# Four rooms for a result tile, a wider step between weight units, and a last sweep in two passes, in a single-core attention and two-layer kernel

## The chip, the cores and the metric

The kernel runs on one core of a Trainium2 chip. The metric is the device time of one execution in microseconds (us), and the number to predict is the median over a few runs. The core has a matrix engine (TensorE, PE in the rows, with its weight loads listed apart as PEld), a vector engine (VectorE, DVE), a scalar engine (ScalarE, ACT), GpSimd (POOL) and SyncE (SP). SyncE computes nothing here; nearly all DMA transfers are issued from its queue (SPq), in the order in which the program writes them, and an issue that has to wait holds back all issues behind it.

## The reference

Attention over 4 batches of 576 tokens and 8 heads of 64 (the first four heads see a band of 32 tokens, the others every 32nd token), and then two small networks on the 2304 tokens:

```python
x = attention(q, k, v)                      # 2304 x 512
h = ((x @ w1) * (x @ w2)) @ w3              # d_ff 1024
y = h @ w_out                               # 2304 x 512
h2 = y @ w_in                               # 2304 x 2048
g = h2 * (1.0 / (1.0 + np.exp(-1.702 * h2)))
out = (g @ w_out2).astype(np.float32)       # 2304 x 512
```

All weights arrive as 8-byte floats.

## The kernel before

**Arithmetic.** Every product of fp32 matrices is made of three matrix multiplications: each factor is split into a rounded part ("hi", written by ScalarE in `split_hi`, L246) and the rest ("lo", written by VectorE in `split_lo`, L252), and `ORDER` lists the three pairs that are multiplied. The product w3 @ w_out is formed once, so y is (a*b) times one matrix. The second network is computed by a scheme with seven block products in place of eight: `win` and `wout` are cut into eight units, the sums of their blocks are formed on the chip and stored in DRAM (`widram` and `tdram`).

**Order.** Four long lists of steps are written by hand. Each step has a number, `written()` sorts a list by these numbers, and what results is the program order of TensorE, VectorE, ScalarE and SyncE. The numbers are places, not times: the engines run as far ahead as their waits for each other allow, each strictly in its own order.

**The third list** (`steps3`, roughly 335 to 437 us) is where most of the change lies. One unit of its numbers is one half piece on TensorE: `one(0)` or `one(1)` in `pieces()`, 12 multiplications (L716) for a 128-column block m of x @ w1 or x @ w2. After `one(0)`, ScalarE copies the result (L1234, `abf<-ps`); after `one(1)`, VectorE multiplies it in (L1237); then ScalarE and VectorE split the product into hi and lo (`ab`). The results of `one` live in the pool `mm`, which has four buffers, so that the half piece four places on needs the copy or the multiplication to be done. For the last of the four batches 16 half pieces (half batch 0), the products for y (`fourth()`, L1354), 16 half pieces (half batch 1) and again `fourth()` follow each other.

Ahead of these stand the last y products of batch 2 (`y_products`, L1173, four tiles n = 0 to 3). `y_out` copies each of the four results to a tile `ysb` (ScalarE, L1181) and stores it (SyncE, L1182). `y_out` takes a tuple of pools, and each pool has two rooms for `ysb`:

```python
ysb = where[n % len(where)].tile([P, HB], F32, tag="ysb", name="ysb", bufs=2)
nc.scalar.activation(ysb, yacc[n], AF.Copy)
nc.sync.dma_start(ydram[n, :, s * HB:(s + 1) * HB], ysb)
```

Between the pieces ScalarE and VectorE do two other jobs. `y_steps` (L1324, L1329 and splits into `yq`) forms the seven block sums of y for the first third of the tokens. `wo_steps` converts one unit of `wout`: two ScalarE steps (L1144, L1145), three VectorE steps (L1146 to L1148), three sums (L1133, L1093, L1133), two ScalarE and two VectorE splits, and two stores of 896 KB each to `tdram` (L1128). Unit 0 goes through `early_room` (tile `x`) with `late` = 1.6, at the end of the second list; units 1 to 6 follow in the third list and use the two halves of `sums` by turns, so a unit waits for the stores of the unit two before it; unit 7 is done in the fourth list. `wo_load` (L1389) loads a unit, 1 MB, into one of three rooms.

**The fourth list** (`steps4`, from 437 us to the end) works on three blocks of 768 tokens. Each has eight `Quad`s, in which the products y @ w_in are made, and then, in `after()`, five sweeps over eight chunks (`piece`, L1508: per chunk three token tiles of 128, three multiplications each). Each sweep takes 8 x 9 multiplications; the split parts come from `Split`, a ring of seven buffers `sp`. The sum of a sweep lies in two PSUM tiles: the first holds token tiles 0 and 1 (512 columns), the second token tile 2 (256 columns). `Out` copies the two or adds them to a room `ob` (L1524, L1529), and `put` stores 384 KB (L1533).

Of the kernel before, what the change touches and what calls it, by code (L numbers as in the profile page):

```python
# [212 lines left out]
def body(ctx: ExitStack, tc, qk, vv, mask, ql, vl, qs, vs, qmask, w1, w2, w3t, wo, win, wout, out):  # L213
# [906 lines left out]
    def wo_steps(u, raw, room, high_room=None, late=0):  # L1120
# [18 lines left out]
        def high(n):  # L1139
# [9 lines left out]
            (2.65, lambda: sum_(S1, B12, B22, ALU.add)),  # L1149
            (2.75, lambda: both_minus(room()[:, 5 * 256:7 * 256], part(B11), room())),  # L1150
            (3.1, lambda: sum_(B12, B21, S2, ALU.add)),
# [101 lines left out]
    for hb in range(2):  # L1253
        for m in range(MC):
            steps2 += pieces(2, hb, m, hold)
        for n in range(KC):
            at_ = 24 * hb + 2 * MC + 2 * n
            todo_ = steps2 if hb == 0 else over
            for half in range(2):
                ks = list(range(4 * half, 4 * half + 4))  # L1260
                todo_.append((at_ + half, lambda hb=hb, n=n, ks=ks: y_products(hb, n, ks)))
            todo_.append((at_ + 1.99, lambda hb=hb, n=n: y_out(4 + hb, n, (p1,))))
# [6 lines left out]
    cv_a = None  # L1269
# [121 lines left out]
    UNIT = 7.2  # L1391
    for u in range(1, NU):
        at = -5.8 if u == 1 else 6 + UNIT * (u - 2)
        if 1 < u < NU - 1:
            steps3.append((((2.6, 5.5, 5.7)[u - 2] if u < 5 else at - 10), lambda u=u: wo_load(u)))
        if u < NU - 1:
            steps3 += [(at + g, f) for g, f in wo_steps(u, lambda u=u: todo3[u], lambda u=u: sums[:, u % 2])]
# [60 lines left out]
    class Split:  # L1458

        def __init__(self, src):  # L1460
            self.src = src

        def hi(self):
            self.t = p2.tile([P, 2, HT], F32R, tag="sp", name="sp", bufs=7)
# [37 lines left out]
    def piece(acc, b, j, i, g, opens=False):  # L1502

        t3 = factor[b, j, i // 2]
        for t in range(HT // P):
# [9 lines left out]
    class Out:  # L1515
# [15 lines left out]
        def put(self, b, right, d):  # L1531
            c0 = b * BT + right * HT
            nc.sync.dma_start(out[c0:c0 + HT, d * 256:d * 256 + 256].rearrange("(t p) n -> p t n", p=P), self.t)  # L1533
# [90 lines left out]
    def after(b, q, X, Y):  # L1624
# [4 lines left out]
        sp = [Split(lambda n=n, i=i: parts[i][:, SWEEP[n][1]]) for n, i in order]  # L1629
        D(PC * 2, piece, Y, b, B21, NU - 1, q.a12, True)  # L1630
        for s, (n, i) in enumerate(order):
            D(PC * pos[s] + 0.01, piece, (X, Y)[n % 2], b, SWEEP[n][0], i, sp[s], n == 1)
# [5 lines left out]
            else:  # L1638
                D(PC * (pos[s] - 3) + 0.1, sp[s].hi)
                D(PC * (pos[s] - 3) + 0.65, sp[s].lo)  # L1640
        D(PC * 3 + 0.02, t_more, 2)
        c11, u1, z1, c22, c21, c12 = (Out() for _ in range(6))
        for n in range(2):
# [6 lines left out]
            D(PC * 41 + 0.02 + 0.01 * n, c12.copy, X, n)  # L1650
# [3 lines left out]
        D(PC * 41 + 0.1, c12.put, b, 0, 1)  # L1654
# [101 lines left out]
```

## Time and profile before

| | |
|---|---|
| median of three runs | 799.18 us (797.74 to 799.43) |
| the profiled execution | 799.78 us |
| span of the profiled execution, first to last instruction | 798.0 us |
| TensorE busy | 771.7 us of the span (97%) |
| VectorE busy | 580.8 us (73%) |
| ScalarE busy | 480.2 us (60%) |
| mean granted TensorE clock, share of full | 0.998 |
| DMA traffic | 168.14 MB, mean 211 GB/s |

The span leaves out 1.78 us of the profiled execution that lie around the first and the last instruction. All times within the execution are counted from the start of the span. TensorE is busy nearly all the time, so what counts is where it is not, and at which clock it runs.

### The profile page before, as it was taken

To read this page: it belongs to the slowest core of one execution; us is meant where nothing else is said; L and a number is where in the kernel's file an instruction comes from. 1 tells how busy PE (TensorE), PEld (TensorE's weight loads), DVE (VectorE), ACT (ScalarE), POOL (GpSimd) and SP (SyncE) were. 2 spreads that over 40 slices of the span, in tenths; PEclk is the share of its full clock that TensorE was granted. 3 is DMA by queue.
4 is the path that set the end of the run, shared out by engine and by line. 5 is a ranking of instruction groups with operands and counts; after the bars stand their busy time and mean duration, and the time that the engine had idled before them with its cause. 6 is when DMAs were issued, how large, how long until landed. Compare 5 with 4: busy or idle time off the path is not lost.

```text
span 798.0 us, 16759 instructions
## 1 busy us (share of the span) xinstructions
PE 771.7 (97%) x6545; PEld 746.6 (94%) x6545; DVE 580.8 (73%) x1248; ACT 480.2 (60%) x1041; POOL 5.8 (1%) x14
## 2 busy tenths in 40 slices
PE   5899999999999999997999999999999999999997
PEld 4889999987999999997989999999999999999997
DVE  4989678788688687967766787795567795577643
ACT  6867646577665545444464667673666673665552
POOL 2000000000000000000000000000000000000000
PEclk9999999999999999999999999999999999999999
DMA  8987455632787545386699936789354489343382
GB/s 261 311 295 240 164 173 185 198 114 82 265 268 278 164 164 217 111 228 212 168 275 261 365 132 204 303 280 361 133 189 166 152 278 364 123 161 108 120 275 82
DMA packets 72062, 168.14 MB, mean 211 GB/s; under 512 B 6320, under 2 KB 45232, under 8 KB 69424
## 3 DMA queue, kind: packets, MB, share of 16 engines
q1 hardware_dynamic: 71840, 167.04, 62.8%
q8 instruction: 51, 0.84, 0.4%
q14 instruction: 27, 0.22, 0.1%
q10 hardware_dynamic: 144, 0.04, 0.0%
HBM read 130.88 MB, written 36.18 MB: 209 GB/s over the span
## 4 chain that ended last, share of the span: by engine, by line
PE 75%; DMA 12%; DVE 6%; ACT 4%; issue 2%; SPq 0%; ACTq 0%; DVEq 0%
PE acc L1508 23%; PE ps L1497 22%; PE ps L716 12%; PE ps L1173 8%; PE acc L1019 5%; DMA raw<-in_w 3%; DMA raw<-in_wout 2%; DMA tdram<-sums 2%; PE acc L1354 2%; DMA ydram<-ysb 1%; DMA vl<-in_vl 1%; PE sc L533 1%; PE pv L602 1%; ACT sm L556 1%; DMA tdram<-raw 1%
## 5 line engine op out<-in xcount | busy, mean ns | idle before, releaser
L1508 PE MATMUL acc<-w,sp 128*128 128x256 f32 x1512 | 188.3, 283 | 0.0
L1508 PEld LDWEIGHTS acc<-w,sp 128*128 128x128 f32 x1512 | 186.5, 191 | 0.1
L1497 PE MATMUL ps<-yq,hl 128*128 128x384 f32 x924 | 168.1, 335 | 0.0
L1497 PEld LDWEIGHTS ps<-yq,hl 128*128 128x128 f32 x924 | 158.7, 188 | 0.9 <-DVE part L1453 0.6
L252 DVE TENSOR_TENSOR sp<-part,sp 128x384 fp32r<-128x384 f32 x144 | 75.3, 552 | 59.9 <-ACT sp L246 59.9
L716 PE MATMUL ps<-xbh,w 128*128 128x288 f32 x512 | 102.6, 295 | 0.8 <-DVE w L252 0.7
L716 PE MATMUL ps<-xah,w 128*128 128x288 f32 x512 | 102.4, 295 | 0.0
L716 PE MATMUL ps<-xal,w 128*128 128x288 f32 x256 | 77.2, 302 | 6.1 <-DVE abf L1237 4.4
L716 PEld LDWEIGHTS ps<-xbh,w 128*128 128x128 f32 x512 | 81.9, 188 | 1.3 <-DVE w L252 1.2
L1173 PE MATMUL ps<-ab,w 128*128 128x288 f32 x576 | 81.0, 300 | 1.8 <-DVE ab L252 1.8
L716 PEld LDWEIGHTS ps<-xah,w 128*128 128x128 f32 x512 | 82.0, 188 | 0.0
L1173 PEld LDWEIGHTS ps<-ab,w 128*128 128x128 f32 x576 | 78.2, 191 | 3.2 <-DVE ab L252 2.2
L716 PE MATMUL ps<-xbl,w 128*128 128x288 f32 x256 | 77.2, 301 | 1.2 <-ACT abf L918 0.8
L246 ACT ACTIVATE sp<-part 128x384 fp32r<-128x384 f32 x144 | 68.2, 518 | 16.4 <-PE acc L1508 15.7
L1450 ACT ACTIVATE part<-part 128x384 f32<-128x384 f32 x72 | 37.9, 526 | 62.2 <-DVE part L1453 62.2
L716 PEld LDWEIGHTS ps<-xal,w 128*128 128x128 f32 x256 | 48.0, 187 | 8.9 <-DVE abf L1237 5.8
L246 ACT ACTIVATE ab<-abf 128x288 fp32r<-128x288 f32 x64 | 27.2, 438 | 44.4 <-DVE abf L1237 40.4
L716 PEld LDWEIGHTS ps<-xbl,w 128*128 128x128 f32 x256 | 48.0, 188 | 2.7 <-ACT abf L918 1.0
L1019 PE MATMUL acc<-w,w 128*128 128x512 f32 x192 | 45.6, 396 | 0.1
L1019 PEld LDWEIGHTS acc<-w,w 128*128 128x128 f32 x192 | 35.8, 188 | 9.2 <-ACT raw L1025 1.0
L252 DVE TENSOR_TENSOR hl<-fetched,hl 128x1024 fp32r<-128x1024 f32 (+1 forms) x40 | 43.2, 1081 | 0.0
L246 ACT ACTIVATE w<-xw 128x512 fp32r<-128x512 f32 (+1 forms) x30 | 23.2, 775 | 29.1 <-DVE xw L809 28.3
(189 smaller groups left out, 1089.1 us busy)
## 6 DMA issues: line engine op xcount, KB each, us to landing
w<-tdram SPq DMA_DIRECT2D x84, 512.0 KB, 4.3
fetched<-widram SPq DMA_DIRECT2D x20, 896.0 KB, 7.4
raw<-in_win SPq DMA_DIRECT2D x8, 1024.0 KB, 5.9
widram<-x SPq DMA_DIRECT2D x8, 896.0 KB, 5.4
raw<-in_wout SPq DMA_DIRECT2D x7, 1024.0 KB, 5.1
tdram<-raw SPq DMA_DIRECT2D x6, 896.0 KB, 6.3
tdram<-sums SPq DMA_DIRECT2D x6, 896.0 KB
raw<-in_w3t SPq DMA_DIRECT2D x10, 512.0 KB, 4.6
```

The source lines that it names most:

```text
L246: nc.scalar.activation(hi, src, AF.Copy)
L252: e.tensor_tensor(lo, src, r(hi), op=ALU.subtract)
L533: nc.tensor.matmul(sc[:nq, g, i * P:i * P + nk], qs[rows, i], ks[rows, i], start=True, stop=True,)
L556: nc.scalar.activation(sm[:nq, h, :nk], sm[:nq, h, :nk], AF.Exp, bias=st[:nq, 0, h:h + 1], scale=-1.0, accum_out=st[:nq, 1, h:h + 1],)
L602: nc.tensor.matmul(pv[rows, h // 2, :nq], L["v"][:nk, h * D:(h + 1) * D], ps[:nk, h * nq:(h + 1) * nq], start=True, stop=True,)
L716: nc.tensor.matmul(ps, ws[a][m // 2][:, at:at + P], xh[c][:, k, cols], start=(k == 0 and (a, c) == ORDER[0]), stop=(k == KC - 1 and (a, c) ...
L1019: nc.tensor.matmul(acc[f], hl[:, a, f * P:(f + 1) * P], wor[c][g], start=(g == 0 and (a, c) == ORDER[0]), stop=(g == MC - 1 and (a, c) == ...
L1173: nc.tensor.matmul(yacc[n], wfs[a][k][:, n * P:(n + 1) * P], hold[s % 2, k][:, c], start=(k == 0 and (a, c) == ORDER[0]), stop=(k == MC - ...
L1354: nc.tensor.matmul(st[0], wfs[a][k][:, n * P:(n + 1) * P], hold[hb, k][:, c], start=(k == 0 and (a, c) == ORDER[0]), stop=(k == MC - 1 and ...
L1450: nc.scalar.activation(out(), src(), func)
L1497: nc.tensor.matmul(ps, w[a][:, f * 256 + kk * P:f * 256 + (kk + 1) * P], yq[:, b, kk, c], start=(first and kk == 0 and (a, c) == ORDER[0]) ...
L1508: nc.tensor.matmul(to, g.t[:, a, t * P:(t + 1) * P], t3[:, i % 2, c], start=(opens and i == 0 and n == 0 and t % 2 == 0), stop=(i == NU - ...
```

## The change

Four edits:

1. The four `y_out` of batch 2's second half batch get the pools `p1` and `cv_b` by turns, so four rooms for `ysb` in place of two.
2. In `wo_steps` the three sums of a unit with `late` (only unit 0, 1.6) get places 0.8 further back.
3. `UNIT`, the distance between two units of `wout` in the third list, is 8.0 in place of 7.2, and the loads of units 5 and 6 stand 14 places ahead of their unit in place of 10.
4. In the last block's last sweep TensorE goes through all eight chunks for token tiles 0 and 1 first, and then through all eight for token tile 2. The eight split parts, which all have to be kept until the end, are written to `yq`, whose contents are no longer needed then, and six chunks ahead in place of three. The first PSUM tile is copied and stored (256 KB) ahead of the end, the second one (128 KB) at the end.

```diff
-            (2.65, lambda: sum_(S1, B12, B22, ALU.add)),
-            (2.75, lambda: both_minus(room()[:, 5 * 256:7 * 256], part(B11), room())),
-            (3.1, lambda: sum_(B12, B21, S2, ALU.add)),
+            (2.65 + late / 2, lambda: sum_(S1, B12, B22, ALU.add)),
+            (2.75 + late / 2, lambda: both_minus(room()[:, 5 * 256:7 * 256], part(B11), room())),
+            (3.1 + late / 2, lambda: sum_(B12, B21, S2, ALU.add)),
...
-            todo_.append((at_ + 1.99, lambda hb=hb, n=n: y_out(4 + hb, n, (p1,))))
+            todo_.append((at_ + 1.99, lambda hb=hb, n=n: y_out(4 + hb, n, (p1, cv_b) if hb else (p1,))))
...
-    UNIT = 7.2
+    UNIT = 8.0
...
-            steps3.append((((2.6, 5.5, 5.7)[u - 2] if u < 5 else at - 10), lambda u=u: wo_load(u)))
+            steps3.append((((2.6, 5.5, 5.7)[u - 2] if u < 5 else at - 14), lambda u=u: wo_load(u)))
...
-            self.t = p2.tile([P, 2, HT], F32R, tag="sp", name="sp", bufs=7)
+            self.t = self.room or p2.tile([P, 2, HT], F32R, tag="sp", name="sp", bufs=7)
...
+        final = b + 1 == NB
+        sp = [
+            Split(lambda n=n, i=i: parts[i][:, SWEEP[n][1]], yq[:, i // 2, i % 2] if final and n == 4 else None) for n, i in order
+        ]
...
+            if final and n == 4:
+                for m, ts in enumerate(((0, 1), (2,))):
+                    D(PC * (33 + (0, 8 * 2 / 3)[m] + i * (2 - m) / 3) + 0.01, piece, X, b, SWEEP[n][0], i, sp[s], False, ts)
...
-                D(PC * (pos[s] - 3) + 0.1, sp[s].hi)
-                D(PC * (pos[s] - 3) + 0.65, sp[s].lo)
+                ahead = 6 if final and n == 4 else 3
+                D(PC * (pos[s] - ahead) + 0.1 + 0.01 * (ahead > 3), sp[s].hi)
+                D(PC * (pos[s] - ahead) + 0.65 + 0.01 * (ahead > 3), sp[s].lo)
...
-            D(PC * 41 + 0.02 + 0.01 * n, c12.copy, X, n)
+            D(PC * (41 - (8 / 3 if final and n == 0 else 0)) + 0.02 + 0.01 * n, c12.copy, X, n)
...
+        if final:
+            D(PC * 41 - 2.5, c12.put, b, 0, 1, 0, 2)
+            D(PC * 41 + 0.1, c12.put, b, 0, 1, 2, 3)
+        else:
+            D(PC * 41 + 0.1, c12.put, b, 0, 1)
```

How edit 2 moves VectorE at the end of the second list (`x` is unit 0; `ab_2714` is the split of the last two blocks, m = 6 and m = 7, of batch 2's second half batch, and each L1237 is the multiplication of one block):

```order
 L1237 TENSOR_TENSOR abf<-ps,abf 128x288
 L252 TENSOR_TENSOR xal<-pv,xah 128x2x96 x2
+L252 TENSOR_TENSOR ab_2714<-abf,ab_2714 128x288
 L1133 TENSOR_TENSOR x<-x 128x256
 L1093 TENSOR_TENSOR x<-x 128x512
 L1133 TENSOR_TENSOR x<-x 128x256
-L252 TENSOR_TENSOR ab_2714<-abf,ab_2714 128x288
 L1237 TENSOR_TENSOR abf<-ps,abf 128x288
 L252 TENSOR_TENSOR ab_2714<-abf,ab_2714 128x288
```

The lo split of block m = 6 moves ahead of the three sums; the multiplication and the split of block m = 7 stay behind them.

How edit 3 moves SyncE's issues, in the third list from the stores of unit 3 on (`raw<-in_wout` are the loads of units 5 and 6; `tdram<-raw` and `tdram<-sums` are the hi and lo stores of units 3 and 5, `tdram<-x` is unit 4's hi store; `w_73` is a block of `w_in`):

```order
-L1128 DMA tdram<-raw 128x7x256
 L1389 DMA raw<-in_wout 128x1024
+L1128 DMA tdram<-raw 128x7x256
 L1128 DMA tdram<-sums 128x7x256
 L1363 DMA ydram<-ysb 128x288 x4
+L1389 DMA raw<-in_wout 128x1024
 L1128 DMA tdram<-x 128x7x256
-L1389 DMA raw<-in_wout 128x1024
-L1128 DMA tdram<-sums 128x7x256
-L1128 DMA tdram<-raw 128x7x256
+L1128 DMA tdram<-sums 128x7x256
```

The load of unit 5 moves ahead of unit 3's hi store, and the load of unit 6 ahead of unit 4's hi store.

How edit 4 moves TensorE at the very end (`w_1624` and `w_1625` are ring buffers with the last factors):

```order
 L1508 MATMUL acc<-w_1627,sp 128x256 x36
-L1508 MATMUL acc<-w_1624,sp 128x256 x36
-L1508 MATMUL acc<-w_1625,sp 128x256 x36
-L1752 UNCONDITIONAL_BRANCH
+L1508 MATMUL acc<-w_1624,yq 128x256 x24
+L1508 MATMUL acc<-w_1625,yq 128x256 x24
+L1508 MATMUL acc<-w_1624,yq 128x256 x12
+L1508 MATMUL acc<-w_1625,yq 128x256 x12
+L1766 UNCONDITIONAL_BRANCH
```

The number of multiplications is the same; a third of them now stands in a second pass. Nowhere else does TensorE's order change.

## Rows read from the trace of the kernel before

**Rows 1.** TensorE in order of time: start, us, instruction, idle time before it

```profile
338.64 0.66 PE L1173 MATMUL ps<-ab,w 128*128 128x288 f32 x3 [1.10 <-DVE ab L252]
339.98 11.71 PE L1173 MATMUL ps<-ab,w 128*128 128x288 f32 x75 [0.67 <-DVE ab L252]
351.53 0.29 PE L716 MATMUL ps<-xal,w 128*128 128x288 f32 x1
...
362.16 0.40 PE L716 MATMUL ps<-xal,w 128*128 128x288 f32 x1 [2.33 <-DVE abf L1237]
...
372.12 0.40 PE L716 MATMUL ps<-xal,w 128*128 128x288 f32 x1 [0.97 <-ACT abf L1234]
...
374.55 0.40 PE L716 MATMUL ps<-xal,w 128*128 128x288 f32 x1 [0.59 <-DVE abf L1237]
...
380.09 0.40 PE L716 MATMUL ps<-xal,w 128*128 128x288 f32 x1 [0.30 <-ACT abf L1234]
```

**Rows 2.** Stretches: length, busy PE, PEld, DVE, ACT, POOL, clock, DMA, GB/s

```profile
341.00:344.00 3.00, 3.00 (x14) 3.00 (x14) 1.88 (x3) 2.49 (x4) 0.00 (x0) 0.50 0.69 196
...
351.50:383.40 31.90, 27.34 (x195) 25.64 (x194) 22.26 (x33) 16.18 (x28) 0.00 (x0) 1.00 0.69 203
...
396.00:424.20 28.20, 26.66 (x196) 25.96 (x195) 20.19 (x32) 14.09 (x24) 0.00 (x0) 1.00 1.01 280
...
436.70:793.80 357.10, 357.10 (x2521) 355.57 (x2519) 247.26 (x407) 217.52 (x400) 0.00 (x0) 1.00 0.61 212
```

**Rows 3.** ScalarE in order of time, 353 to 372 us

```profile
353.65 0.41 ACT L1181 ACTIVATE ysb<-ps 128x288 f32<-128x288 f32 x1 [4.22 <-DMA ydram<-ysb]
...
369.30 1.14 ACT L1144 ACTIVATE raw<-raw 128x1024 int32<-128x1024 uint32 x1 [2.28 <-DMA raw<-in_wout]
...
371.69 0.38 ACT L1234 ACTIVATE abf<-ps 128x288 f32<-128x288 f32 x1
```

**Rows 4.** VectorE in order of time, 338 to 374 us

```profile
338.14 0.45 DVE L252 TENSOR_TENSOR ab<-abf,ab 128x288 fp32r<-128x288 f32 x1
338.51 0.45 DVE L1237 TENSOR_TENSOR abf<-ps,abf 128x288 f32<-128x288 f32 x1
339.47 0.46 DVE L252 TENSOR_TENSOR ab<-abf,ab 128x288 fp32r<-128x288 f32 x1 [0.51 <-ACT ab L246]
...
354.94 1.09 DVE L252 TENSOR_TENSOR sums<-sums,raw 128x896 fp32r<-128x896 f32 x1 [4.38 <-ACT raw L246]
...
361.66 0.45 DVE L1237 TENSOR_TENSOR abf<-ps,abf 128x288 f32<-128x288 f32 x1
...
374.05 0.45 DVE L1237 TENSOR_TENSOR abf<-ps,abf 128x288 f32<-128x288 f32 x1
```

**Rows 5.** The chain of work that ended last: start, us, what

```profile
344.31 9.26 DMA ydram<-ysb
353.96 0.95 ACT raw L246
354.93 5.48 DMA tdram<-raw
360.43 8.77 DMA raw<-in_wout
...
393.01 13.19 DMA tdram<-sums
...
424.16 12.58 PE acc L1354 x96
```

**Rows 6.** Two stretches with little DMA: length, clock, DMA share, GB/s

```profile
376.00:380.00 4.00, 1.00 0.00 0
...
388.00:392.00 4.00, 1.00 0.01 3
```

**Rows 7.** ScalarE's last two copies, in order of time

```profile
793.50 0.87 ACT L1524 ACTIVATE ob<-acc 128x512 f32<-128x512 f32 x2 [6.67 <-PE acc L1508]
```

**Rows 8.** The last stretches, columns as in the second group

```profile
795.00:796.00 1.00, 0.00 (x0) 0.00 (x0) 0.00 (x0) 0.00 (x0) 0.00 (x0) 1.00 0.69 236
796.00:797.00 1.00, 0.00 (x0) 0.00 (x0) 0.00 (x0) 0.00 (x0) 0.00 (x0) 1.00 0.47 158
```

More of the change, by code (lines that the diff above doesn't have):

```diff
@@ L1268, in body @@
     right2 = ExitStack()
-    cv_a = None
+    cv_a = cv_b = None
     early = {}
@@ L1458, in body, with __init__ @@
     class Split:
-        def __init__(self, src):
-            self.src = src
+        def __init__(self, src, room=None):
+            self.src, self.room = src, room
         def hi(self):
-            self.t = p2.tile([P, 2, HT], F32R, tag="sp", name="sp", bufs=7)
+            self.t = self.room or p2.tile([P, 2, HT], F32R, tag="sp", name="sp", bufs=7)
             split_hi(self.t[:, 0], self.src())
@@ L1500, in product, with piece @@
                 )
-    def piece(acc, b, j, i, g, opens=False):
+    def piece(acc, b, j, i, g, opens=False, ts=range(HT // P)):
         t3 = factor[b, j, i // 2]
-        for t in range(HT // P):
+        for t in ts:
             to = acc[t // 2][:, t % 2 * 256:t % 2 * 256 + 256]
@@ L1529, in add, with put @@
             nc.vector.tensor_tensor(self.o[:, WIDE[n]], acc[n][:, :768 - 512 if n else 512], other.o[:, WIDE[n]], op=ALU.add)
-        def put(self, b, right, d):
+        def put(self, b, right, d, lo=0, hi=HT // P):
             c0 = b * BT + right * HT
-            nc.sync.dma_start(out[c0:c0 + HT, d * 256:d * 256 + 256].rearrange("(t p) n -> p t n", p=P), self.t)
+            nc.sync.dma_start(
+                out[c0 + lo * P:c0 + hi * P, d * 256:d * 256 + 256].rearrange("(t p) n -> p t n", p=P), self.t[:, lo:hi]
+            )
     MM, PC = 1.05, 1.07
@@ L1628, in after @@
         pos = [s if s < 2 else s + 1 for s in range(len(order))]
-        sp = [Split(lambda n=n, i=i: parts[i][:, SWEEP[n][1]]) for n, i in order]
+        final = b + 1 == NB
+        sp = [
+            Split(lambda n=n, i=i: parts[i][:, SWEEP[n][1]], yq[:, i // 2, i % 2] if final and n == 4 else None) for n, i in order
+        ]
         D(PC * 2, piece, Y, b, B21, NU - 1, q.a12, True)
         for s, (n, i) in enumerate(order):
-            D(PC * pos[s] + 0.01, piece, (X, Y)[n % 2], b, SWEEP[n][0], i, sp[s], n == 1)
+            if final and n == 4:
+                for m, ts in enumerate(((0, 1), (2,))):
+                    D(PC * (33 + (0, 8 * 2 / 3)[m] + i * (2 - m) / 3) + 0.01, piece, X, b, SWEEP[n][0], i, sp[s], False, ts)
+            else:
+                D(PC * pos[s] + 0.01, piece, (X, Y)[n % 2], b, SWEEP[n][0], i, sp[s], n == 1)
             if i % 2:
@@ L1653, in after @@
         D(PC * 33 + 2.4, c21.put, b, 1, 0)
-        D(PC * 41 + 0.1, c12.put, b, 0, 1)
+        if final:
+            D(PC * 41 - 2.5, c12.put, b, 0, 1, 0, 2)
+            D(PC * 41 + 0.1, c12.put, b, 0, 1, 2, 3)
+        else:
+            D(PC * 41 + 0.1, c12.put, b, 0, 1)
         if b + 1 < NB:
```

## Prediction

> **What bounds the kernel now.** I first read the stretches. From 436.7 us on TensorE is busy for all of 357.1 us at full clock [rows 2], so the fourth list is bound by TensorE, and what starts it earlier ends it earlier by the same amount. The third list is different. Twelve multiplications, a half piece, take 12.58 / 96 x 12 = 1.57 us where nothing waits [rows 5], so 16 of them take 25.2 us. Half batch 0 takes 31.9 us and half batch 1 takes 28.2 us [rows 2]: 6.7 and 3.0 us are waits and restarts. Then I read who ends them. TensorE's own order shows it idle for 2.33, 0.97, 0.59 and 0.30 us ahead of half pieces that need a PSUM buffer back, from a copy (ACT L1234) or a multiplication (DVE L1237) [rows 1]. VectorE and ScalarE lead further back: the multiplication that ended the 2.33 us stood at 361.66 behind work that began after an idle 4.38 us at 354.94 [rows 4], and that waited for ScalarE, which had stood 4.22 us for the store of a `ysb` tile [rows 3]. The chain of waits puts these in one line: store of `ysb` 9.26 us, split, `tdram` store 5.48, load of unit 2 8.77, and later a `sums` store of 13.19 us [rows 5]. So there it is a chain of transfers, not TensorE, that sets the time.
>
> A smaller loss comes earlier: TensorE waits 1.10 and 0.67 us for the lo splits of blocks m = 6 and 7 [rows 1], and from 341 to 344 us the granted clock is 0.50, the level of 1.2 GHz, which costs half of 3.0 us, 1.5 us [rows 2].
>
> **Edit 1, the rooms.** It removes the 4.22 us. The third copy can begin at 353.65 - 4.22 = 349.4; its result is there by then, since the fourth tile's 24 multiplications (3.1 us) end at 351.5 [rows 1], so the third's ended at 348.4. In the built order the second and fourth copies wait for TensorE alone and the third for a store of the half batch before: the new rooms are free. Queued behind the third copy are the split at 353.96, the splits of y, the fourth copy and the first copies of half batch 0; all move 4.2 us. On VectorE the multiplication at 361.66 comes at 357.4 and ends at 357.9. TensorE wants its buffer at 362.16 - 2.33 = 359.8: the 2.33 us are gone.
>
> What is late next is unit 2. Its load waits for unit 1's hi store (same room). That store goes out at 350.7 instead of 354.93; with the same 5.48 and 8.77 us [rows 5] the unit is there at 365.0, where ScalarE took it up at 369.30 after idling 2.28 us [rows 3]. ScalarE's copy of block 3 stands behind the unit's two conversions: 371.69 becomes 367.4, done at 367.8; TensorE, running from 351.53 without waits, wants it after ten half pieces at 367.2, and waits 0.6. The multiplication of block 3, 374.05 [rows 4], becomes 369.8 and ends at 370.2; wanted at 369.4, a wait of 0.8. The copy that released TensorE at 380.09 [rows 1] does so at 375.8; wanted at 370.2 + 3 x 1.57 = 374.9, 0.9. So 2.3 us of the 6.7 remain, and half batch 0 ends about 4.3 us earlier, as much as the transfers move. Bounds: were the store to take the longest landing seen, 13.19 us, the load would come after 369.3 and nothing is won; were both transfers shorter, all 6.7 us. I take the same transfers' own times, 4.3 us, as sizes and neighbours are the same.
>
> **Edit 3, the distance of the units.** In half batch 1 the waits came from unit 5, whose second conversion could not write `sums` until unit 3's store had landed, 393.01 + 13.19 = 406.2 us [rows 5]. That store shared the DMA engines with the load of unit 5, issued just before. Now that load stands ahead of unit 3's stores; it waits only for unit 2's hi store to land, at about 375.1 + 5.5 = 380.6, and the engines are nearly idle then (shares of 0.00 and 0.01 in two stretches [rows 6]). Unit 3's lo store goes out near 393.0 - 4.3 = 388.7 and lands at 394.2 (5.48 us) or 401.9 (13.19 us). Unit 5's conversion stands 6.1 places into half batch 1, which begins at 396.0 - 4.3 = 391.7: 401.3. So even the longest landing leaves 0.6 us, and ScalarE and VectorE have some 3 us in hand ahead of the PSUM buffers. Of the 3.0 us I take 2.8; the bounds are 0 (another wait takes its place) and 3.0. Behind the moved loads on SyncE stand the stores of units 3 and 4. Their cover: unit 3's hi store isn't due until 388, 7 us after the load in front can go. The load of unit 6, ahead of unit 4's stores, waits for unit 3's hi store; if it lands late, unit 4's stores wait, and only unit 6's conversion 12 us later waits for them.
>
> **Edit 2, the sums.** Block 6's lo split moves from 338.14 to 336.7, and TensorE's first wait of 1.10 us goes. But block 7's multiplication stays behind the three sums at 338.51, and its split at 339.47 is what lets TensorE go on at 339.98 [rows 1, 4]. The two short waits become one of about 2.1 us that ends at the same place, some 0.1 us later as one more instruction stands in front. I count a loss of 0.1 us. The low clock from 341 us followed these waits; the wait of 2.33 us at 359.8 was followed by no fall, the clock of that stretch is 1.00 [rows 2]. So rows alone don't decide whether the fall comes again; I keep it, with 1.5 us either way in the range. The Trainium skill (TensorE: Matmul & The Clock Gate, Part 1) says that the monitor that gates the clock runs freely, so that the same kernel meets it at another phase in each run. By that rule the 1.5 us is there in some runs and not in others; one profile can't show it.
>
> **Edit 4, the last sweep.** The multiplications are the same in number and form. Each chunk's split stands six places ahead; the first pass takes two thirds of a place per chunk, so the last chunk has 37.7 - 34.7 = 3 places, as all chunks had before. No room has to come free for them, and TensorE's last 357 us show no wait, so I count nothing there; without that cover a chunk would wait about 1 us. The gain lies behind TensorE's last multiplication. There ScalarE made two copies in 0.87 us [rows 7]; now one of 256 columns, at most the 0.38 us of a copy of 288 [rows 3]: 0.5 us. The store then moved 394 KB in 0.69 + 0.47 = 1.16 us of the engines' time [rows 8]; a third of it is left: 0.8 us less, since the 256 KB go out 2 us earlier, under TensorE. Together 1.2 us, between 0.5 (the transfer costs the same) and 1.3. The Trainium skill (DMA: Bandwidth & Descriptors, Anatomy of one DMA) speaks against splitting a store: each carries a fixed cost of about 2 us and 436 KB per us after it. By it the last store saves 256 / 436 = 0.6 instead of 0.8 us, an estimate, and the fixed part is paid twice, the first time beside TensorE's second pass.
>
> **The sum.** 4.3 + 2.8 + 1.2 - 0.1 = 8.2 us. Against the profiled execution: 799.78 - 8.2 = 791.6 (span 798.0, and 1.78 around it). The median of the runs shown is 0.6 lower, which would give 791.0. I forecast 791.3.
>
> **The rivals.**
> - *All waits of the third list go.* If unit 2 lands 2 us earlier than I have it, the remaining 2.3 us vanish too: 799.8 - 6.7 - 3.0 - 1.2 = 788.9, and 787.4 without the low clock. For it: the load at 360.43 shared the engines with unit 1's lo store. Against: it still does.
> - *The transfers don't move.* Unit 1's store at 350.7 meets the load of y, in flight with the `ysb` stores until 353.6 [rows 5]. If unit 2 is only 1 to 2 us earlier, TensorE waits longer at its copy, and in half batch 1 a new wait for a store may take the place of the old: 799.8 - 1.5 - 1.4 - 1.2 = 795.7, between 793.3 and 797.5.
> - *The rooms change nothing*, because the copy then waits for something else. Then only the last store is won, 798.4, no change that counts. The 3.1 us between the tiles and the built order speak against it.
> - *Slower: SyncE's queue is held.* Unit 5's load, now ahead of unit 3's stores, waits for unit 2's hi store. Once unit 3's lo store lands after 404 us, TensorE loses one for one. To eat 8.2 us the store must land at 412, so unit 2's hi store near 406, 31 us after its issue, more than twice the longest of 13.19 us. At 35 us the time would be 803.
>
> **How the numbers follow.** The forecast's own case (790.0 to 793.3) gets 0.50, no waits left 0.18, transfers that move little 0.24, rooms without effect 0.04, slower 0.04. The range goes from 788.0 to 796.0: it leaves out some 0.04 below, and above it a third of the third case (0.08) and the last two (0.08). A change of 0.2% is 1.6 us, about what a measurement of this kernel can tell from none; faster by more than that 0.92, within it 0.04, slower 0.04.
>
> **What would show it.** Right: no idle time on ScalarE ahead of the third `ysb` copy, unit 2's first conversion near 365, TensorE's remaining waits in half batch 0 about 2.3 us, none in half batch 1, the fourth list starting near 429.7, one wait of 2.1 us near 338, and a last copy of 256 columns. Wrong: unit 2 near 369; a wait for `tdram<-sums` in half batch 1; waits of the first `Quad`s for `hl` or the ring, as the last units' stores end closer to them than before; idle TensorE in the last sweep.

## Result and profile after

The changed kernel takes 792.2 us (median of six runs, 790.30 to 793.06); the kernel before took 800.22 us in the runs beside it (797.74 to 802.63). The ratio is 0.9898, 95% interval [0.9875, 0.9921]: 8.0 us, or 1.0%, faster. The kernel before is 1.0 us slower in these six runs than in the three that the prediction started from (799.18 us), so most of the distance to the forecast of 791.3 us lies in the base and not in the change. The profiled execution took 791.2 us, with a span of 789.4 us and a mean granted TensorE clock of 0.996.

The two profiles differ by 8.6 us, and not all of that is the change. The first of the last y products (L1173) starts at 334.04 us now and started at 335.01 before, though nothing that lies ahead of it was changed: 0.97 us of the difference is how long the opening happened to take. Below, times of the two traces are therefore compared as distances from this multiplication or from one another.

TensorE in order of time (start, us, instruction, idle time before it and what ended it), from the wait for block 7 to the fourth list, in the changed kernel:

```profile
339.09 11.73 PE L1173 MATMUL ps<-ab,w 128*128 128x288 f32 x75 [2.12 <-DVE ab L252]
350.67 0.29 PE L716 MATMUL ps<-xal,w 128*128 128x288 f32 x1
...
366.99 0.40 PE L716 MATMUL ps<-xal,w 128*128 128x288 f32 x1 [0.36 <-ACT abf L1234]
...
369.41 0.40 PE L716 MATMUL ps<-xal,w 128*128 128x288 f32 x1 [0.58 <-DVE abf L1237]
...
374.95 0.40 PE L716 MATMUL ps<-xal,w 128*128 128x288 f32 x1 [0.30 <-ACT abf L1234]
...
378.21 12.85 PE L1354 MATMUL acc<-ab,w 128*128 128x288 f32 x96
...
416.50 12.85 PE L1354 MATMUL acc<-ab,w 128*128 128x288 f32 x96
...
429.20 11.93 PE L1497 MATMUL ps<-yq,w 128*128 128x384 f32 x66
```

Of the waits of [rows 1] the 2.33 us are gone, 0.97 has become 0.36, and 0.59 and 0.30 are still there; a wait of 0.37 us at 369.31 that those rows leave out is gone too. Half batch 0 takes 378.21 - 350.67 = 27.5 us, where it took 31.9 [rows 2]. Between the two L1354 rows no wait is left. The two short waits at the top have become the one of 2.12 us that the prediction named.

The chain of work that ended last (start, us, what) through the same stretch:

```profile
349.73 7.20 DMA tdram<-raw
356.95 7.10 DMA raw<-in_wout
...
378.38 12.69 PE acc L1354 x96
391.06 25.60 PE ps L716 x192
...
429.36 6.25 PE ps L1497 x36
```

In [rows 5] this chain ran through the store of a `ysb` tile (9.26 us) and later through a store of `sums` (13.19 us). Both are gone from it. What is left is unit 1's store and unit 2's load with its conversion, and from 378 us on nothing but TensorE. The fourth list starts at 429.36, before at 436.74: 7.4 us earlier, 6.4 without the opening.

ScalarE in order of time, at the rooms and at unit 2:

```profile
348.47 0.39 ACT L1181 ACTIVATE ysb<-ps 128x288 f32<-128x288 f32 x1
...
364.15 1.14 ACT L1144 ACTIVATE raw<-raw 128x1024 int32<-128x1024 uint32 x1 [2.33 <-DMA raw<-in_wout]
```

The third copy to `ysb` runs straight behind a split, with no idle time; in [rows 3] it had stood for 4.22 us. Unit 2's first conversion is at 364.15, still idle 2.33 us for its load, and 5.2 us earlier than before (4.2 without the opening).

VectorE in order of time, at block 7:

```profile
335.73 0.46 DVE L252 TENSOR_TENSOR ab<-abf,ab 128x288 fp32r<-128x288 f32 x1
...
337.62 0.45 DVE L1237 TENSOR_TENSOR abf<-ps,abf 128x288 f32<-128x288 f32 x1
338.58 0.46 DVE L252 TENSOR_TENSOR ab<-abf,ab 128x288 fp32r<-128x288 f32 x1 [0.51 <-ACT ab L246]
```

Block 6's lo split now stands ahead of the sums, at 335.73 where it was at 338.14 [rows 4]; block 7's multiplication and split come 0.89 us earlier than before, which is a little less than the opening gave. So the edit gained nothing here.

Stretches (length, busy time of the engines, clock, share of the DMA engines, GB/s):

```profile
341.00:342.00 1.00, 1.00 (x6) 1.00 (x5) 0.52 (x1) 1.00 (x3) 0.00 (x0) 0.50 0.80 268
350.70:378.20 27.50, 26.25 (x193) 25.36 (x193) 21.66 (x34) 14.88 (x26) 0.00 (x0) 1.00 0.73 232
390.90:416.50 25.60, 25.60 (x194) 25.60 (x193) 19.18 (x31) 15.91 (x27) 0.00 (x0) 1.00 0.97 279
429.40:786.30 356.90, 356.88 (x2520) 355.49 (x2518) 246.00 (x407) 216.30 (x398) 0.00 (x0) 1.00 0.61 213
787.00:788.00 1.00, 0.00 (x0) 0.00 (x0) 0.00 (x0) 0.00 (x0) 0.00 (x0) 1.00 0.37 123
788.00:789.00 1.00, 0.00 (x0) 0.00 (x0) 0.00 (x0) 0.00 (x0) 0.00 (x0) 1.00 0.03 8
```

The clock still falls to 0.50 (1.2 GHz) behind the wait for block 7. Half batch 1 has TensorE busy in all of its 25.6 us. From the first multiplication of the fourth list to TensorE's last one it takes 357.1 us, and 357.2 before. The last store needs 0.37 + 0.03 = 0.40 us of the DMA engines' time, where it needed 1.16 [rows 8].

ScalarE's last two copies:

```profile
783.47 0.60 ACT L1524 ACTIVATE ob<-acc 128x512 f32<-128x512 f32 x1 [10.30 <-PE acc L1508]
786.34 0.38 ACT L1524 ACTIVATE ob<-acc 128x256 f32<-128x256 f32 x1 [2.28 <-PE acc L1508]
```

Only the second, of 256 columns, stands behind TensorE's last multiplication, which ends at 786.31. From there to the end of the span it is 3.1 us. In the kernel before it was 4.2 us. The chain of work leaves TensorE there at 793.48, but that is the end of token tiles 0 and 1, for which the first copy waits [rows 7]; the three multiplications for token tile 2 still run beside that copy, until 793.82, so that 0.57 us of ScalarE's 0.87 lie behind them. The stretch after 793.80 in the kernel before (columns as above):

```profile
793.80:798.00 4.20, 0.02 (x1) 0.00 (x0) 0.00 (x0) 0.57 (x2) 0.00 (x0) 1.00 0.28 94
```

So edit 4 wins 1.1 us here. The 4.5 us in the expectations of e3_sweep and e5_one_store count from 793.48, not from the last multiplication.

### The profile page after: what moved, and what is told of

Its sections match the earlier page's. It is cut to its first block, busy times and chain, and to the rows that moved or that the text cites. A ratio compares the mean times of both kernels' runs of the same rounds, so it can differ in the third digit from the quotient of the medians.

```text
span 789.4 us, 16754 instructions
## 1 busy us (share of the span) xinstructions
PE 770.6 (98%) x6545; PEld 747.6 (95%) x6545; DVE 580.8 (74%) x1248; ACT 480.2 (61%) x1041; POOL 5.8 (1%) x14
## 4 chain that ended last, share of the span: by engine, by line
PE 84%; DMA 5%; DVE 4%; ACT 4%; issue 1%; SPq 1%; ACTq 0%; DVEq 0%
PE acc L1508 23%; PE ps L1497 22%; PE ps L716 20%; PE ps L1173 8%; PE acc L1354 3%; PE acc L1019 3%; PE sc L533 1%; DMA sums<-ydram 1%; PE pv L602 1%; DMA tdram<-raw 1%; DMA raw<-in_wout 1%; ACT w L246 1%; DVE w L252 1%; DVE xw L809 1%; ACT xw L801 1%
## 5 line engine op out<-in xcount | busy, mean ns | idle before, releaser
L1508 PE MATMUL acc<-w,sp 128*128 128x256 f32 x1440 | 179.5, 282 | 0.0
L1508 PEld LDWEIGHTS acc<-w,sp 128*128 128x128 f32 x1440 | 177.8, 191 | 0.0
L1497 PE MATMUL ps<-yq,hl 128*128 128x384 f32 x924 | 168.1, 335 | 0.0
L1497 PEld LDWEIGHTS ps<-yq,hl 128*128 128x128 f32 x924 | 158.7, 188 | 0.9 <-DVE part L1453 0.6
L252 DVE TENSOR_TENSOR sp<-part,sp 128x384 fp32r<-128x384 f32 x136 | 71.5, 554 | 59.1 <-ACT sp L246 59.1
L1173 PE MATMUL ps<-ab,w 128*128 128x288 f32 x576 | 80.7, 300 | 2.2 <-DVE ab L252 2.1
L1173 PEld LDWEIGHTS ps<-ab,w 128*128 128x128 f32 x576 | 78.2, 191 | 3.3 <-DVE ab L252 2.4
L246 ACT ACTIVATE sp<-part 128x384 fp32r<-128x384 f32 x136 | 64.1, 517 | 11.3 <-PE acc L1508 10.3
```

The costliest lines, as they stand in the source:

```text
L246: nc.scalar.activation(hi, src, AF.Copy)
L252: e.tensor_tensor(lo, src, r(hi), op=ALU.subtract)
L1173: nc.tensor.matmul(yacc[n], wfs[a][k][:, n * P:(n + 1) * P], hold[s % 2, k][:, c], start=(k == 0 and (a, c) == ORDER[0]), stop=(k == MC - ...
L1497: nc.tensor.matmul(ps, w[a][:, f * 256 + kk * P:f * 256 + (kk + 1) * P], yq[:, b, kk, c], start=(first and kk == 0 and (a, c) == ORDER[0]) ...
L1508: nc.tensor.matmul(to, g.t[:, a, t * P:(t + 1) * P], t3[:, i % 2, c], start=(opens and i == 0 and n == 0 and t % 2 == 0), stop=(i == NU - ...
```

## Experiments

The question was whether the time came from where the sum put it. Theory A: the transfers that edits 1 and 3 move were on the path, so each edit wins its own term, the terms add up, and the wait at block 7 with the low clock behind it is slack, because what follows waits for transfers anyway. Each expectation states it in numbers, with its rivals.

This table cuts each profiled execution in two: from the first of the last y products (L1173) to the first multiplication of the fourth list (L1497), and from there to TensorE's last one. It leaves out the opening, which varies from run to run. e3_sweep alters nothing ahead of the fourth list; its 102.3 beside the 101.6 of before shows how far single profiles spread. e5_one_store has the third list of the changed kernel, and 94.3 beside 95.2. So less than 1 us in this column can't be told from none.

| kernel | ratio to before, 95% interval | median, us | third list, us | fourth list, us |
|---|---|---|---|---|
| before | | 800.22 | 101.6 | 357.2 |
| after | 0.9898 [0.9875, 0.9921] | 792.20 | 95.2 | 357.1 |
| e1_rooms | 0.9945 [0.9926, 0.9963] | 796.92 | 96.7 | 357.4 |
| e2_units | 0.9969 [0.9955, 0.9984] | 797.99 | 98.6 | 357.1 |
| e3_sweep | 0.9984 [0.9969, 1.0000] | 799.39 | 102.3 | 357.3 |
| e4_sums | 1.0000 [0.9983, 1.0016] | 801.05 | 101.9 | 357.5 |
| e5_one_store | one run | 792.06 | 94.3 | 357.1 |
| e6_block7 | 0.9900 [0.9874, 0.9925] | 792.20 | 94.9 | 358.4 |
| e7_unit2 | 1.0006 [0.9991, 1.0021] | 801.14 | 92.9 | 368.5 |
| e8_both | 1.0005 [0.9989, 1.0021] | 800.93 | 92.9 | 368.3 |
| e9_unit2_75 | 0.9911 [0.9881, 0.9942] | 793.84 | 92.2 | 361.4 |
| e10_all | 0.9908 [0.9881, 0.9935] | 792.74 | 93.2 | 358.0 |
| e11_units70 | 0.9913 [0.9886, 0.9940] | 793.40 | 95.2 | 357.1 |
| e12_all70 | 0.9898 [0.9876, 0.9920] | 792.90 | 95.7 | 357.7 |

The runs of before beside the experiments had medians of 800.46 (e1 to e4), 800.54 (e5 to e8), 800.89 (e9, e10) and 800.64 us (e11, e12).

### The four edits alone

**e1_rooms**, the kernel before with edit 1 alone:

```diff
-            todo_.append((at_ + 1.99, lambda hb=hb, n=n: y_out(4 + hb, n, (p1,))))
+            todo_.append((at_ + 1.99, lambda hb=hb, n=n: y_out(4 + hb, n, (p1, cv_b) if hb else (p1,))))
```

> Edit 1 alone: four rooms for the results of batch 2's second half batch, all else as before. Theory A (the wait for a room started a chain of transfers that set TensorE's time in half batch 0; half batch 1 has a chain of its own, through unit 3's stores): ScalarE's 4.22 us ahead of the third copy are gone, unit 2's first conversion comes 4 to 5 us earlier, half batch 0 takes 27.5 to 28.5 us instead of 31.8, half batch 1 stays near 28.1, in all 4 us faster. Rival B (the wait in half batch 1 was only the late end of the same chain): half batch 1 falls to 25.6 us as well, in all 6.5 us faster. Rival C (the room wait is hidden by something else): no change.

Measured: 0.9945, or 4.4 us faster by the ratio; the medians lie 3.5 us apart. TensorE in order of time:

```profile
342.55 10.10 PE L1173 MATMUL ps<-ab,w 128*128 128x288 f32 x75 [0.68 <-DVE ab L252]
...
380.96 12.85 PE L1354 MATMUL acc<-ab,w 128*128 128x288 f32 x96
...
408.83 0.40 PE L716 MATMUL ps<-xal,w 128*128 128x288 f32 x1 [0.63 <-DVE abf L1237]
...
411.12 0.40 PE L716 MATMUL ps<-xal,w 128*128 128x288 f32 x1 [0.44 <-ACT abf L1234]
...
413.46 0.40 PE L716 MATMUL ps<-xal,w 128*128 128x288 f32 x1 [0.47 <-DVE abf L1237]
```

Half batch 0 takes 28.5 us, with the waits of the changed kernel in it and without the 2.33 us; the three waits of half batch 1 are still there. So the rooms act on half batch 0 alone. In this run the clock didn't fall behind block 7: 75 multiplications in 10.10 us in place of 11.71 [rows 1].

**e2_units**, the kernel before with edit 3 alone:

```diff
-    UNIT = 7.2
+    UNIT = 8.0
...
-            steps3.append((((2.6, 5.5, 5.7)[u - 2] if u < 5 else at - 10), lambda u=u: wo_load(u)))
+            steps3.append((((2.6, 5.5, 5.7)[u - 2] if u < 5 else at - 14), lambda u=u: wo_load(u)))
```

> Edit 3 alone: units of w_out 8.0 apart, the loads of units 5 and 6 further ahead, two rooms as before. Theory A: half batch 0 stays at 31.8 us, since unit 2 keeps its place and the 4.2 us for the room stay; half batch 1 falls from 28.1 to 25.6 us, in all 2.5 us faster. Rival B (without the rooms the spacing does nothing): half batch 1 stays near 28.1, no change.

Measured: 0.9969, or 2.5 us faster. TensorE in order of time:

```profile
363.21 0.40 PE L716 MATMUL ps<-xal,w 128*128 128x288 f32 x1 [2.34 <-DVE abf L1237]
...
383.56 12.86 PE L1354 MATMUL acc<-ab,w 128*128 128x288 f32 x96
421.86 12.85 PE L1354 MATMUL acc<-ab,w 128*128 128x288 f32 x96
```

Half batch 0 keeps its 2.34 us, and half batch 1 has no wait: 38.3 us from one group of y products to the next, as in the changed kernel (38.3), where the kernel before took 40.6. So edit 3 doesn't need the rooms. Unit 3's lo store, for which unit 5 waited before, lands 9.9 us after its issue here, where it took 13.19 [rows 5], and ScalarE doesn't wait for it. Which of the edit's two parts does it, the distance or the earlier loads, was not tried apart.

**e3_sweep**, the changed kernel with edits 1, 2 and 3 undone:

```diff
-            (2.65 + late / 2, lambda: sum_(S1, B12, B22, ALU.add)),
+            (2.65, lambda: sum_(S1, B12, B22, ALU.add)),
...
-            todo_.append((at_ + 1.99, lambda hb=hb, n=n: y_out(4 + hb, n, (p1, cv_b) if hb else (p1,))))
+            todo_.append((at_ + 1.99, lambda hb=hb, n=n: y_out(4 + hb, n, (p1,))))
...
-    UNIT = 8.0
+    UNIT = 7.2
...
```

and likewise for the other two sums and the loads of units 5 and 6.

> Edit 4 alone: the last sweep in two passes, its split parts in the place of y, the last results stored in two parts. From TensorE's last multiplication to the end of the span 3.1 us instead of 4.5, TensorE without a wait in the last sweep, in all 1.4 us faster. Rival (the fixed part of a store dominates, and the splits are late in the first pass): 4.0 us or more from the last multiplication to the end, or idle time of TensorE in the last sweep, no change.

Measured: 0.9984, or 1.3 us, at the edge of what the runs can tell. The end of the chain:

```profile
773.96 18.97 PE acc L1508 x158
...
792.95 0.38 ACT ob L1524
```

The span ends at 796.0 us, 3.1 us after the last multiplication (792.92), as in the changed kernel; in the kernel before it was 4.2. The multiplications of the last sweep form one group without idle time.

**e4_sums**, the kernel before with edit 2 alone:

```diff
-            (2.65, lambda: sum_(S1, B12, B22, ALU.add)),
+            (2.65 + late / 2, lambda: sum_(S1, B12, B22, ALU.add)),
```

and likewise for the other two sums.

> Edit 2 alone: the three sums of unit 0 behind the split of block 6. Theory A: TensorE's two waits of 1.10 and 0.67 us become one of 2.1 us that ends at the same place, no change in the total; half batch 0 is bound by transfers in this kernel, so even a fall of the clock behind the wait costs nothing. Rival: the one longer wait brings or removes the low clock, and the total moves by 1.5 us either way.

Measured: 1.0000, no change. TensorE in order of time:

```profile
340.28 10.19 PE L1173 MATMUL ps<-ab,w 128*128 128x288 f32 x75 [2.12 <-DVE ab L252]
...
354.34 0.40 PE L716 MATMUL ps<-xal,w 128*128 128x288 f32 x1 [0.69 <-ACT ysb L1181]
...
356.62 0.40 PE L716 MATMUL ps<-xal,w 128*128 128x288 f32 x1 [0.43 <-ACT ysb L1181]
...
362.38 0.40 PE L716 MATMUL ps<-xal,w 128*128 128x288 f32 x1 [2.34 <-DVE abf L1237]
```

This run says more than its ratio. The clock didn't fall, so the 75 multiplications took 1.5 us less than in [rows 1]; but then TensorE waited 0.69 and 0.43 us for `ysb` copies, which it had not done there, and from the wait at block 7 to the first L1354 (340.28 to 384.13) it took 43.9 us, no less than the 43.4 of before. In the kernel before, the clock's 1.5 us lay in slack. (The ratio alone can't show this: it is taken over all runs, and where the clock fell is known for the profiled one only.)

The four ratios lie 0.55, 0.31, 0.16 and 0.00% under one; together 1.02%, and the whole change measures 1.02%. The edits add up, as theory A had it, within what the runs can tell: the intervals are 0.15 to 0.23 of a percent to either side, so that the two figures agree to the last digit is luck.

### The last store

**e5_one_store**, the changed kernel with one store of 384 KB at the end:

```diff
-            D(PC * 41 - 2.5, c12.put, b, 0, 1, 0, 2)
-            D(PC * 41 + 0.1, c12.put, b, 0, 1, 2, 3)
+            D(PC * 41 + 0.1, c12.put, b, 0, 1)
```

> The changed kernel, but the last results go out in one store of 384 KB again, behind the second copy; sweep and copies stay. It takes the shorter store of edit 4 apart from its shorter copy. Theory A (the transfer's time is by its size): the copies' part, 0.5 us, stays, the store's part is lost; 4.0 us from TensorE's last multiplication to the end (3.1 in the changed kernel, 4.5 before). Rival (the store's fixed part is all): 3.1 us.

Measured in one run: the last multiplication ends at 786.26 and the span at 790.3, 4.0 us later, where the changed kernel has 3.1 and the kernel before 4.2. The last stretches with DMA:

```profile
787.00:788.00 1.00, 0.00 (x0) 0.00 (x0) 0.00 (x0) 0.00 (x0) 0.00 (x0) 1.00 0.38 128
788.00:789.00 1.00, 0.00 (x0) 0.00 (x0) 0.00 (x0) 0.00 (x0) 0.00 (x0) 0.67 0.79 265
```

So of the 1.1 us at the end, 0.9 is the smaller store and 0.2 the copy; theory A has the store right, and the copy's 0.5 us is refuted. The engines' busy time falls by 1.17 - 0.40 = 0.77 us, about what the prediction took (0.8); the other 0.1 us lies outside that busy time.

### What the remaining waits are worth

**e6_block7**, the changed kernel with unit 0's sums behind block 7's lo split as well:

```diff
-            (2.65 + late / 2, lambda: sum_(S1, B12, B22, ALU.add)),
+            (2.65 + late * 1.07, lambda: sum_(S1, B12, B22, ALU.add)),
...
-    steps2 += [(EARLY_AT + g, f) for g, f in wo_steps(0, lambda: early[0], early_room, None, 1.6)]
+    steps2 += [(EARLY_AT + g, f) for g, f in wo_steps(0, lambda: early[0], early_room, None, 2.4)]
```

and likewise for the other two sums.

> The changed kernel with the three sums of unit 0 behind block 7's multiplication and split too, so that TensorE need not wait 2.1 us for them. Theory A (half batch 0 is bound by transfers, TensorE's earlier loss is slack): TensorE goes on 1.5 us earlier and its waits in half batch 0 grow by as much or more; unit 1 comes 0.6 us later; the total stays within 0.7 us of the changed kernel. Rival B (TensorE bounds this stretch): 1.5 us faster than the changed kernel, 3.2 us where the low clock goes as well.

Measured: 792.2 us, the changed kernel's own median. TensorE in order of time:

```profile
339.71 10.10 PE L1173 MATMUL ps<-ab,w 128*128 128x288 f32 x75 [0.61 <-DVE ab L252]
...
354.99 0.40 PE L716 MATMUL ps<-xal,w 128*128 128x288 f32 x1 [0.44 <-ACT ysb L1181]
...
359.76 0.40 PE L716 MATMUL ps<-xal,w 128*128 128x288 f32 x1 [1.35 <-DVE abf L1237]
```

The wait at block 7 shrinks from 2.12 to 0.61 us and the clock stays full, 3.1 us together; 0.44 and 1.35 us appear further on, and the third list is only 0.3 us shorter. Unit 0's sums are now later, and with them its store, unit 2's load and the y steps. This is slack being given back, as theory A had it. But the 1.35 us come ahead of unit 2's load, for a multiplication that VectorE makes behind the block sums of y; e8_both shows more of this.

**e7_unit2**, the changed kernel with units 2 to 6 two places later, so that the copies of half batch 0 don't stand behind unit 2:

```diff
-        at = -5.8 if u == 1 else 6 + UNIT * (u - 2)
+        at = -5.8 if u == 1 else 8 + UNIT * (u - 2)
```

> The changed kernel with units 2 to 6 two places later, so that ScalarE makes the copy of block 3 before it waits for unit 2's load. Theory A (in-order ScalarE, held by the load, is what is left of TensorE's waits): no waits of TensorE in half batch 0, which takes 25.6 us instead of 27.5, 2 us faster than the changed kernel. Rival B (the waits move to the next unit or to the products behind): the half batch or the stretch to the fourth list takes as long as before.

Measured: 801.14 us; the whole gain of the change is lost. Half batch 0 does run without a wait (352.24 to 377.52, 25.3 us), and the third list is 2.3 us shorter. But the fourth list is 11 us longer. TensorE there, and then ScalarE, in order of time:

```profile
433.01 6.00 PE L1497 MATMUL ps<-yq,w 128*128 128x384 f32 x24 [2.24 <-ACT s L1562]
...
443.26 7.06 PE L1497 MATMUL ps<-yq,w 128*128 128x384 f32 x30 [4.26 <-DVE part L1453]
```

```profile
428.00 1.79 ACT L246 ACTIVATE raw<-sums 128x896 fp32r<-128x896 f32 x2 [7.17 <-DVE sums L1133]
...
441.63 0.52 ACT L246 ACTIVATE sp<-part 128x384 fp32r<-128x384 f32 x1 [4.13 <-DMA ydram<-ysb]
```

Unit 6 is now the last thing before the fourth list. ScalarE stands 7.17 us for its sums, the splits come at 428.00, and behind them queue the last copies to `ysb`; the first steps of the fourth list wait for the stores of those tiles. The clock fell as well (0.83 from 430 to 450 us). Half batch 0 behaved as theory A has it; this place it had missed.

**e8_both**, e6_block7 and e7_unit2 together.

> Both of these in the changed kernel. Theory A (the load of unit 2 hides what edit 2 could win): with the load off TensorE's way, block 7's earlier split counts now: 2 us faster than the changed kernel from the units and 1.5 from the split, 3.5 us in all, up to 5 where the low clock goes. Rival B (the 1.5 us stay hidden behind another transfer): 2 us faster, as the units alone.

Measured: 800.93 us. It loses in the same place (fourth list 368.3 us). Theory A failed: from the first L1173 to the first L1354 it takes 41.9 us here and 41.9 in e7_unit2, so all that is won at block 7 is given back in half batch 0, though unit 2's load is out of the way. TensorE, and then the chain of work that leads there:

```profile
358.38 0.40 PE L716 MATMUL ps<-xal,w 128*128 128x288 f32 x1 [1.31 <-DVE abf L1237]
```

```profile
342.99 8.94 DMA tdram<-x
...
352.16 0.95 DVE x L1324
...
357.88 0.45 DVE abf L1237
```

The multiplication that TensorE wants stands behind y's block sums on VectorE. These go into tile `x`, which unit 0's lo store reads (the first row); that store moved back with unit 0's sums, and VectorE itself is busy with unit 1 until about the time it lands. So it is another transfer, as rival B had it, and VectorE's work beside it; which of the two would hold TensorE alone was not tried.

**e9_unit2_75**, e7_unit2 with the units closer together, so that unit 6 stands where the changed kernel has it (place 38):

```diff
-    UNIT = 8.0
+    UNIT = 7.5
```

> The changed kernel with unit 2 two places later, but the units 7.5 apart, so that unit 6 stands where it stands in the changed kernel. The last attempt with all units two places later lost 9 us at the start of the fourth list while half batch 0 had no wait. Theory A (that loss came from unit 6 alone, whose late steps held up the copies of the last y results; half batch 0 is won): half batch 0 takes 25.5 us, the fourth list starts without waits, 2 us faster than the changed kernel. Rival B (the load of the DMA engines at that place does it, wherever unit 6 stands): waits of several us in the first Quads again.

Measured: 793.84 us, 0.9911: no better than the changed kernel. The third list is 3 us shorter and the fourth 4.3 us longer. ScalarE and then TensorE at its start:

```profile
435.79 0.49 ACT L1562 ACTIVATE z<-ps 128x384 f32<-128x384 f32 x1 [2.98 <-DMA ydram<-ysb]
```

```profile
436.34 8.08 PE L1497 MATMUL ps<-yq,w 128*128 128x384 f32 x36 [2.00 <-ACT z L1562]
```

The next bound is the landing of the last four `ysb` stores. SyncE issues them behind unit 6's two stores of 896 KB (424.45 and 426.50 us, with the fourth list at 428.96; in the changed kernel 422.69 and 424.74, with 429.20). Less than 2 us decide whether the fourth list waits. This holds for the profiled execution, which at 795.28 us was one of the slower ones of six that lie between 789.51 and 795.86; whether the faster ones had the wait is not known.

**e10_all**, e9_unit2_75 with block 7 ahead of unit 0's sums, as in e6_block7, and one y step 0.2 places later:

```diff
-    for kk, at in ((1, -0.9), (0, 2.2)):
+    for kk, at in ((1, -0.7), (0, 2.2)):
```

> The same, with unit 0's three sums behind block 7's split, and y's first block sums 0.2 places later, so that the fourth y copy and the first multiplication of half batch 0 stand ahead of the last splits of y on ScalarE and VectorE. Theory A (TensorE's loss near 338 us counts once nothing else in half batch 0 makes it wait): TensorE goes on 1.5 us earlier there and half batch 0 stays near 25.5 to 26.5 us, 1 to 1.5 us faster than the variant with the units alone, up to 3 where the low clock goes. Rival B (the transfers still set the place): waits in half batch 0 grow by what is won, no difference between the two.

Measured: 792.74 us, 0.9908: the same again, and not to be told from e9_unit2_75. Theory A's gain isn't there: half batch 0 takes 28.9 us, with 1.79 us of waiting at 361.89 for a multiplication of VectorE behind y's block sums, as in e8_both. TensorE comes to the fourth list 1.0 us later than in e9_unit2_75, counted from the first L1173, and its wait there is smaller, 0.48 us.

**e11_units70** takes the units of e7_unit2 closer still, so that unit 6 is at place 36 and its stores leave earlier:

```diff
-        at = -5.8 if u == 1 else 6 + UNIT * (u - 2)
+        at = -5.8 if u == 1 else 8 + UNIT * (u - 2)
...
-    UNIT = 8.0
+    UNIT = 7.0
```

> The changed kernel, with the units of w_out from place 8 on and 7.0 places apart, so that unit 6 stands at place 36 and its two stores are issued some 3 us earlier than in e9_unit2_75. Theory A (the start of the fourth list waits for the last stores of y, which queue behind the two stores of unit 6): no wait for ydram<-ysb at the start of the fourth list, half batch 0 of the third list in about 26 us, about 2 us faster than the changed kernel, near 790. Rival B (units this close together bring back the waits of the second half batch, as 7.2 did in the kernel before): half batch 1 takes 28 us where the changed kernel takes 25.6, and the time is no better than the changed kernel's 792.

Measured: 793.4 us, 0.9913. Both mechanisms were there, and rival B gave the time. Theory A's part: no wait for `ydram<-ysb`, a fourth list of 357.1 us, and half batch 0 in 25.3 us (351.09 to 376.38) without a wait. Rival B's: ScalarE and TensorE in half batch 1, in order of time,

```profile
403.73 1.28 ACT L1405 ACT_TABLE_LOAD   x1
```

```profile
405.58 0.40 PE L716 MATMUL ps<-xal,w 128*128 128x288 f32 x1 [0.42 <-ACT abf L1234]
...
410.00 0.40 PE L716 MATMUL ps<-xal,w 128*128 128x288 f32 x1 [0.65 <-ACT abf L1234]
...
424.57 5.38 PE L1354 MATMUL acc<-ab,w 128*128 128x288 f32 x39 [0.37 <-DVE ab L252]
```

The table load, which the changed kernel has at 402.05, stands between unit 5's conversion and the copies that TensorE waits for. From the wait at block 7 to the first L1354 it takes 36.7 us in place of 39.1, and from there to the fourth list 53.4 in place of 51.0: 2.4 us won and 2.4 given back.

**e12_all70**, e11_units70 with the two shifts of e10_all: block 7 first, and the y step at -0.7 in place of -0.9, so 0.2 places later (the expectation words this shift wrongly).

> e11_units70 with the sums of unit 0 behind the low half of block 7 and the y steps of the second chunk 0.7 places earlier, as in e10_all. Theory A: as e11_units70, and 1 to 3 us less where nothing else waits at the start of the fourth list, so 787 to 789. Rival B: waits of the second half batch as in e11_units70; what is won at block 7 is given back there, and the time is 791 to 793.

Measured: 792.9 us, 0.9898, the changed kernel's own ratio; here too the waits of half batch 1 are back (0.25, 0.44 and 0.65 us), and half batch 0 takes 28.2 us where e11_units70 took 25.3. Rival B was right on both counts. No version beat the changed kernel.

## Why the prediction was right

It said 791.3 us (range 788.0 to 796.0); 792.2 was measured. Step by step, with what the traces show:

- **Edit 1, 4.3 us.** Half batch 0 went from 31.84 to 27.54 us, 4.3 us, and alone the edit measures 4.4 by the ratio, with an interval of 1.5 us either way. The mechanism is the one given: no idle time before the third copy, and unit 2 as what is late next. Its two transfers were both mis-sized, and the errors cancelled: the store took 7.20 us where 5.48 was taken, the load 7.10 where 8.77 was, 14.30 in place of 14.25 together. That they cancelled is luck. The floor was right: 16 half pieces of half batch 0 without a wait take 25.3 us (e7_unit2, e11_units70), so of the 2.3 us that were to remain 2.2 do, of which 1.24 are idle time in the rows above.
- **Edit 3, 2.8 us.** From the first L1354 to the fourth list it is 53.2 us before and 51.0 after, so 2.2 us; alone the edit measures 2.5. All waits went, as forecast; the term was too large at both ends: half batch 1 took 27.9 us before, the 28.2 being the length of the stretch that was looked at, and its floor is 25.6 us and not 25.2. Unit 3's lo store landed 9.7 us after its issue, between the two times that were taken. None of the new waits feared behind the moved loads came: unit 5's load goes out at 379.94, unit 3's stores follow at 387.28 and 388.56.
- **Edit 2, a loss of 0.1 us.** From the first L1173 to where TensorE goes on it is 4.97 us before and 5.05 after. Alone the edit measures 1.0000.
- **Edit 4, 1.2 us.** 1.1 us in the profile (4.2 to 3.1), 1.3 alone by the ratio. The copy was mis-sized: the two copies of 0.87 us began while TensorE was still at its last three multiplications, so that 0.2 us were to be won and not 0.5. The smaller store won 0.9 rather than 0.8 us (e5_one_store). The last sweep has no idle time.
- **The low clock, kept, with 1.5 us either way.** It did come again. The range counted it as worth 1.5 us, and that was wrong: e4_sums had no fall in its profile and reached the first L1354 no sooner, and e6_block7 had neither the fall nor most of the wait and was no faster either. What holds half batch 0 is the `ysb` store before, unit 2's load in the changed kernel, and unit 0's store and VectorE's work in e8_both; time won ahead of them turns into waiting in it.

The terms that the traces show add up to 7.5 us, the medians differ by 8.0, and the interval of the ratio is 1.8 us to either side, so the total is no finer check than that. One more reading was off: 13.19 us is not the longest landing in the trace of before, where the store of `sums` issued at 402.92 took 13.97.

The rivals fell: the transfers did move, SyncE's queue was not held, and some waits of half batch 0 stayed. The case in which all waits go was built in e7_unit2 and e11_units70, and shows what the prediction's 788.9 us left out: taking half batch 0 down to its floor moves units later or closer together, and the time is given back at the start of the fourth list or in half batch 1. Which of VectorE and ScalarE would have to be relieved first in half batch 1 for e11_units70 to keep its 2.4 us was not tried, nor was a version in which unit 0's store and y's block sums no longer meet in tile `x`.

## What to carry to other kernels

Where a stage is set by a chain of transfers, follow the chain and price what comes next in it; the gain of a removed wait is how far the next transfer moves, not the length of the wait. Waits and low clock that lie ahead of such a chain are slack, so shortening them buys nothing until the chain is shorter, and then the next holder has to be looked for: behind unit 2's load it was another store, and VectorE's own work. And when a unit of background work is moved, look at its last instance too: here the stores of the last unit, two places later, stood in front of the stores that the next stage waits for, and cost more than the whole change had won.

## What the hardware showed that was not expected

The clock's fall to 0.50 behind the wait at block 7 comes and goes from profile to profile. With one wait of 2.12 to 2.16 us it fell in the profiles of after, e5_one_store, e7_unit2 and e11_units70 (75 multiplications in 11.62 to 11.73 us) and did not in e4_sums and e9_unit2_75 (10.19 and 10.10); with waits of 1.10 and 0.67 us it fell in before, e2_units and e3_sweep and did not in e1_rooms. With 0.60 to 0.64 us (e6_block7, e8_both, e10_all, e12_all70) it did not fall in any. The Trainium skill (TensorE: Matmul & The Clock Gate, Part 1) says of the slow stretch at a kernel's start that the monitor behind the gate runs freely and that its effect varies between runs of one kernel. These profiles show such a variation in mid-kernel: after, e5_one_store, e7_unit2, e9_unit2_75 and e11_units70 run the same instructions up to this place, and the clock fell in four of the five.

The store at the very end was worth more than its bytes. Leaving 256 KB out of it won 0.9 us (4.0 to 3.1 us behind TensorE's last multiplication, e5_one_store beside the changed kernel). The Trainium skill (DMA: Bandwidth & Descriptors, Anatomy of one DMA) gives 436 KB per us behind a fixed part, fitted to transfers that GpSimd issues, while this store is issued by SyncE. By it 256 KB are 0.6 us, an estimate; here the measurement decides, 0.9 us.
